# A linear-attention recurrence with a top-1 mixture of experts behind it: fewer matmuls of zeros, later weight splits, whole-block input loads, a new order at the seam

## The chip, the core and the metric

The kernel runs on one core of a Trainium2 chip. A core has five engines that run side by side: TensorE (PE in the profile, its weight loads PEld), VectorE (DVE), ScalarE (ACT), GpSimd (POOL) and SyncE (SP), which here only issues DMA transfers. The metric is the device time of one execution in microseconds (us), the median of the runs shown.

## The reference

Two layers follow one another. The first runs over time; the second sends each of the 3072 tokens to one of eight experts.

```python
B, H, S, D = 4, 8, 768, 48              # batch, heads, time, head width
for t in range(S):
    cur = einsum('bhd,bhe->bhde', u * k[t], v[t])
    y[t] = einsum('bhd,bhde->bhe', r[t], state + cur)
    state = w[t][..., None] * state + einsum('bhd,bhe->bhde', k[t], v[t])
x = y as [3072, 384]
logits = x @ w_gate                      # 8 experts
e = argmax(logits); gate = max(softmax(logits))
out[token] = gate * (relu(x @ w1[e]) @ w2[e])   # w1 384x1024, w2 1024x384
```

## The kernel before

**Blocks.** Time is cut into six chunks of 128 steps. A block is one chunk of one batch row, so there are 24 blocks, n = 0 to 23, chunk n // 4, batch row n % 4. The eight heads stand in pairs: partitions 0 to 47 hold the even heads and 64 to 111 the odd ones, so tiles have 112 rows (`RP`). `iteration(n)` issues a software pipeline on TensorE, VectorE, ScalarE and GpSimd, in an order that is written out by hand: products of decays by scans for block n+2 (`pre`, `suf`), from them `rh` and `kh` (VectorE), `rk` = r times k for block n+3 (GpSimd), the matrix `ap` = kh by rh for block n (`pe_a`), its causal part written into `at` (`dve_at`), the part of the state (`pe_inter`), the output (`pe_av`), the new state (`pe_state`), and for block n-1 the transposed output (`pe_y`). The loop runs over n = -3 to 21; the last two blocks, 22 and 23, are written out behind it.

**Matmuls of zeros.** `keep_warm` multiplies a tile of ones with a tile of zeros into a part of a bank that nobody reads. It stands ahead of the loop (`WARM`: 40 of 128 columns, 24 of 512), in `pe_coef` (384 columns) and in `pe_state` (320 columns).

**Routing.** When a chunk's four blocks are done, `logit_mm`, `gate`, `count`, `rank` and `place` find each token's expert and row, and `scatter` writes the rows to `xs` in DRAM, sorted by expert, by an indirect DMA from GpSimd for each block. For the last chunk this is done block by block (`pe_logits`, `gate`, `rank`, then `chosen` = place, weigh, scatter).

**Experts.** Weights are kept as a high and a low part (`split_piece`: ScalarE copies the high part, VectorE subtracts for the low one), and a product of two such numbers is three matmuls. An expert's weights come in four pieces of 128 by 1536; each piece is split in three parts of 512 columns. Expert 0 is split during the loop, one part per block from block 8 on (`split_piece(*lows[0], half="h")`, the low half one block later). Its first 192 tokens, the part `pa`, are worked on at the end of the recurrence: `load_rows`, three steps of `transpose_rows`, eight `mm1(f)`, then `mm2`. The other 256 tokens are the part `pb`: its rows can be loaded only when all scatters have landed. Then come experts 1 to 7, sorted by their token counts.

**Queues.** Every load is issued by SP in program order. A load waits for its buffer and stops all that stand behind it. The staging pool `wst` has three buffers, so a piece of weights can be loaded when the piece three before it has been split. Blocks of inputs go round a ring of six buffers (`ld`); from block 6 on, a block's w, r and k come in two transfers of 48 rows, which leave out the unused rows:

```python
for rs in ((slice(None),) if n < LD else (slice(0, D), slice(64, RP))):
    nc.sync.dma_start(t[rs], rkw[n][rs])
```

Of the kernel before, what the change touches and what calls it, by code (L numbers as in the profile page):

```python
# [19 lines left out]
P = 128  # L20
C = 128
# [6 lines left out]
NR = NP_ * C  # L28
NTOK = B * S
# [8 lines left out]
WARM = (40, 24)  # L38
# [7 lines left out]
def rwkv_moe_kernel(ctx, tc, rkw, vv, ub, wgp, wg, w1, w2, out):  # L46
# [26 lines left out]
    def load(n):  # L73
        if n >= NB:
            return

        if n < LD:
            ring.append(ld.tile([RP, NW + 2 * NR], F32, name="rkwt", tag="rkwt"))
        t = ring[n % LD]
        if n == 0:  # L80
            for cs in (slice(0, NW), slice(NW, NW + NR), slice(NW + NR, NW + 2 * NR)):
                nc.sync.dma_start(t[:, cs], rkw[n][:, cs])
        else:
            for rs in ((slice(None),) if n < LD else (slice(0, D), slice(64, RP))):
                nc.sync.dma_start(t[rs], rkw[n][rs])
        blk[n] = dict(
            w=t[:, 0:NW], r=t[:, NW:NW + NR].rearrange("p (q c) -> p q c", c=C),
            k=t[:, NW + NR:].rearrange("p (q c) -> p q c", c=C))

# [100 lines left out]
    def load_piece(e, i):  # L190
        st = (ld if (e, i) == (SECOND, 3) else wst).tile([P, 1536], F32, name="wst", tag="rkwt" if (e, i) == (SECOND, 3) else "wst")
        if i < 2:
            src = w1[e].rearrange("e (j p) (k f) -> p (e j) k f", p=P, f=512)
            for q in range(3):
                lin = 3 * i + q
                nc.sync.dma_start(st[:, q * 512:(q + 1) * 512], src[:, lin // 2, lin % 2, :])
        else:
            src = w2[e].rearrange("e (c p) d -> p (e c) d", p=P)
            nc.sync.dma_start(st.rearrange("p (c d) -> p c d", d=DM), src[:, 4 * (i - 2):4 * (i - 2) + 4, :])
        return st  # L200
# [13 lines left out]
    def w1v(t, pt, j, f):  # L214
        col = j * FF + f * P
        return t["w1", pt].rearrange("p a b -> p (a b)")[:, col:col + P]
# [44 lines left out]
    def transpose_rows(t, nq, rows, xh, xl):  # L261
        for j in range(3):
# [46 lines left out]
    def pool_rk(n):  # L309
        if real(n):  # L310
            d = blk[n]
            d["rk"] = wk.tile([RP, NP_, C], F32, name="rk", tag="rk", bufs=4)
            i = nc.gpsimd.tensor_tensor(out=d["rk"], in0=d["r"], in1=d["k"], op=ALU.mult)  # L313
# [47 lines left out]
    def dve_at(n):  # L361
        if real(n):
            d = blk[n]
            for j in range(2):
                nc.vector.copy_predicated(out=d["at"][:, j], mask=cmask.unsqueeze(1).broadcast_to([P, NP_, C]), data=d["ap"][j])  # L365
# [20 lines left out]
    def act_y(n):  # L386
        if real(n):
            d = blk[n]
            yt = ytb[n % NY]
            if n >= B:  # L390
                nc.scalar.activation(yt, d["yp"], AF.Copy)
# [31 lines left out]
    def pe_coef(n):  # L423

        if real(n):
            t = psL.tile([P, BANK], F32, name="cp", tag="lg")
            keep_warm(t[:, C:], 6 if n < B else 3 if n % B in (2, 3) else 1)
# [39 lines left out]
    def pe_state(n):  # L467
        if real(n) and n // B < NCH - 1:
# [3 lines left out]
            keep_warm(t[:, NP_ * D:], 6 if n < B else 2 if n % B < 2 else 0)  # L472
# [172 lines left out]
    def scatter(c, bs=range(B)):  # L645
        xr = ch["xr", c]
        for b in bs:
            i = nc.gpsimd.indirect_dma_start(out=xsf, out_offset=bass.IndirectOffsetOnAxis(ap=ch["pi", c, b], axis=0),  # L648
                                             in_=xr[:, b, :], in_offset=None, bounds_check=E * NTOK - 1, oob_is_err=False)
            for k in scat:  # L650
                tc.declare_no_dep(i.ins, k, reason="rows of different tokens")
            scat.append(i.ins)

            nc.gpsimd.memset(none, 0.0)
# [5 lines left out]
    class Part:  # L660
# [8 lines left out]
        def trans(self):  # L669
            weights(self.t)  # L670
            transpose_rows(self.t, 2, self.rows, self.x[0], self.x[1])
# [17 lines left out]
    lows = []  # L689

    def iteration(n):
# [7 lines left out]
        whole = (route, 0, B)  # L699
        act_y(n - 1)  # L700
# [5 lines left out]
        pool_rk(n + 3)  # L706
        if n in (6, 7):
            scatter(0, (2 * n - 12,))
# [4 lines left out]
        if n in (6, 7):  # L713
            scatter(0, (2 * n - 11,))
        if route > 0 and b > 1:
            scatter(route, (2 * b - 4, 2 * b - 3))
# [9 lines left out]
        dve_rh(n + 2)  # L726
        act_xr(n - 1)
# [15 lines left out]
        if n < NB - 3:  # L743
            dve_kh(n + 2)
        for k in lows:
# [6 lines left out]
        if route >= 0 and b == 1 and not last:  # L752
# [3 lines left out]
        if 0 <= m < 12:  # L756
# [12 lines left out]
        if n in (14, 17, 20, 21):  # L769
            stg[1, (14, 17, 20, 21).index(n)] = load_piece(SECOND, (14, 17, 20, 21).index(n))  # L770
# [104 lines left out]
    with tc.manual_schedule(engines={ET.PE, ET.DVE, ET.Activation, ET.Pool}):  # L875
# [9 lines left out]
        def chosen(i):  # L885
            place(each[i])
            weigh(each[i])
            scatter(lc, (i,))
# [3 lines left out]
        dve_at(n2)  # L892
        pool_diag(n3)
# [3 lines left out]
        dve_kh(n3)  # L897
        act_xr(n2 - 1)
        place((lc - 1, 0, B))
        scatter(lc - 1)  # L900
        pe_av(n2)
        act_y(n2)
        gate(each[0])
        count(each[0])
        pe_a(n3)
        pe_logits(n2 - 1)
        act_ex(each[0])
        pe_inter(n3)
        dve_at(n3)
# [4 lines left out]
        count(each[1])  # L914
        pe_av(n3)
        act_y(n3)
        act_ex(each[1])
        pe_logits(n2)
        chosen(0)
        pa.trans()  # L920
        rank(each[1])
        gate(each[2])
# [6 lines left out]
        banks = [(psA, "ap"), (psA, "ap"), (psK, "kp"), (psK, "kp")]  # L929
        pa.mm1(0)  # L930
# [5 lines left out]
        pa.mm1(1)  # L936
        pa.mm1(2)
        rank(each[3])
        chosen(3)
        pa.mm1(3)  # L940
        sort_experts()
        check_w()
        pa.mm1(4)
        pa.mm1(5)
        check()
# [3 lines left out]
        pa.mm1(6)  # L949
        pa.mm1(7)  # L950
# [35 lines left out]
def general(tc, rkw, vv, wg, w1, w2, out, xs, ident, tri, ones, ubt, iom, ebase, tokid, dram):  # L986
# [6 lines left out]
    with ExitStack() as st:  # L993
# [22 lines left out]
        with ExitStack() as s1:  # L1016
            gp = s1.enter_context(tc.tile_pool(name="g2", bufs=1))
            gps = s1.enter_context(tc.tile_pool(name="g2p", bufs=1, space=PSUM))
            with tc.For_i(0, NB, 1) as n:
                blk = bass.ds(n, 1)  # L1020
                t = gp.tile([RP, NW + 2 * NR], F32, name="grkw")
                nc.sync.dma_start(t, rkw[blk].rearrange("o p f -> p (o f)"))
# [150 lines left out]
```

## Time and profile before

| | |
|---|---|
| median of 3 runs | 431.68 us (431.0 to 433.52) |
| the profiled execution's own time | 432.07 us |
| its span, first to last instruction | 430.4 us |
| PE, PEld | 417.7 us (97%), 369.6 us (86%) |
| DVE, ACT, POOL | 272.7 us (63%), 222.2 us (52%), 130.1 us (30%) |
| mean granted TensorE clock | 0.973 of full speed |
| DMA | 62.62 MB, mean 146 GB/s |

The recurrence takes the first 168 us of the span, part `pa` and the end of the routing some 25 us behind it, and the rest are the experts. Busy shares are means over all of this; PE's records overlap, so that its share tells little by itself. The profiled execution is 0.39 us over the median.

### The profile page before, as it was taken

The numbers are of one execution on the slowest core, as the hardware profiler recorded it, in microseconds if no ns is written. First come the engines' busy times: TensorE is split into PE (matmuls) and PEld (weight loads), VectorE is DVE, ScalarE is ACT, GpSimd is POOL, SyncE is SP. The second block draws the span as 40 slices with busy tenths as digits, with TensorE's granted clock in tenths as the row PEclk, the third lists the DMA queues.
The fourth block names the chain that finished last, engine by engine and source line by source line (L and its number), as shares of the span: only waits on it lengthen the run. The fifth ranks groups of instructions, "written<-read, shape, count | busy, mean of one in ns | idle before, by whom it ended". The sixth has DMA issues, their size and how long they took to land.

```text
span 430.4 us, 9690 instructions
## 1 busy us (share of the span) xinstructions
PE 417.7 (97%) x3693; PEld 369.6 (86%) x3693; DVE 272.7 (63%) x499; ACT 222.2 (52%) x629; POOL 130.1 (30%) x160
## 2 busy tenths in 40 slices
PE   8999999999999998999999999999999999999994
PEld 5677778777777787989999988899999999999993
DVE  6999888998999974346874364364463562632321
ACT  4689687787887762135563353353363543421310
POOL 3654175463744634101010030031030071020432
PEclk9999999999999998579999999999999999999998
DMA  8999986885974152154862463454365435010021
GB/s 219 252 214 281 246 226 178 217 217 132 270 189 131 39 176 109 40 135 142 261 203 68 142 183 89 144 160 121 131 191 143 148 91 158 14 51 2 6 42 60
DMA packets 33179, 62.62 MB, mean 146 GB/s; under 512 B 8086, under 2 KB 21199, under 8 KB 33126
## 3 DMA queue, kind: packets, MB, share of 16 engines
q1 hardware_dynamic: 25222, 52.41, 44.9%
q0 software_dynamic: 7904, 9.52, 7.2%
q8 instruction: 31, 0.51, 0.6%
q14 instruction: 22, 0.18, 0.1%
HBM read 50.03 MB, written 12.29 MB: 145 GB/s over the span
## 4 chain that ended last, share of the span: by engine, by line
PE 54%; issue 34%; POOL 4%; DMA 3%; ACT 3%; DVE 1%; POOLq 0%; ACTq 0%
PE bank L274 10%; PE ap L452 5%; PE yp L464 5%; PE yp L488 5%; POOL out_dram L236 4%; PE opt L291 4%; DMA out_dram<-ot,xg 3%; PE yq L495 3%; PE bank L859 3%; PE dp L479 2%; PE kp L443 2%; PE cp L111 2%; PE wrm L111 2%; PE cp L429 2%; PE cpt L435 2%
## 5 line engine op out<-in xcount | busy, mean ns | idle before, releaser
L236 POOL DMA_INDIRECT out_dram<-ot,xg x24 | 35.2, 1469 | 157.2 <-DVE ot L849 151.7
L212 DVE TENSOR_TENSOR w2l<-wst,w2h 128x512 fp32r<-128x512 f32 x48 | 31.5, 686 | 44.3 <-ACT w2h L210 44.1
L274 PE MATMUL bank<-xl,w1h 128*128 128x448 f32 (+6 forms) x168 | 59.0, 355 | 0.0
L274 PE MATMUL bank<-xh,w1l 128*128 128x448 f32 (+6 forms) x168 | 58.2, 352 | 0.0
L274 PE MATMUL bank<-xh,w1h 128*128 128x448 f32 (+6 forms) x168 | 55.7, 359 | 0.6 <-ACT xh L266 0.3
L277 DVE SCALAR_TENSOR_TENSOR hl<-bank,hh 128x192 fp32r<-128x192 f32 (+8 forms) x58 | 30.5, 540 | 36.3 <-ACT hh L276 36.3
L313 POOL TENSOR_TENSOR rk<-rkwt 112x512 f32<-112x512 f32 x24 | 32.8, 1368 | 65.5 <-DVE suf L344 48.0
L276 ACT ACTIVATE hh<-bank 128x192 fp32r<-128x192 f32 (+8 forms) x58 | 26.6, 477 | 47.3 <-PE bank L274 43.5
L864 ACT ACTIVATE oT<-bank 128x448 f32<-128x448 f32 (+5 forms) x18 | 9.4, 525 | 61.6 <-PE bank L859 61.6
L859 PE MATMUL bank<-hl,w2h 128*128 128x412 f32 (+5 forms) x114 | 40.6, 358 | 0.0
L859 PE MATMUL bank<-hh,w2l 128*128 128x412 f32 (+5 forms) x114 | 40.4, 356 | 0.0
L859 PE MATMUL bank<-hh,w2h 128*128 128x412 f32 (+5 forms) x114 | 40.0, 357 | 0.0
L365 DVE COPY_PREDICATED at<-cmask,ap 128x512 f32<-128x512 int32 x48 | 32.4, 727 | 9.6 <-PE ap L452 7.1
L350 DVE TENSOR_TENSOR_SCAN suf<-rkwt,suf 112x520 f32<-112x520 f32 x24 | 33.6, 1398 | 0.0
L648 POOL DMA_INDIRECT xs<-xr,pi x24 | 27.6, 1149 | 19.6 <-DVE xr L553 6.9
L274 PEld LDWEIGHTS bank<-xh,w1h 128*128 128x128 f32 x168 | 31.2, 188 | 2.2 <-ACT xh L266 0.7
L274 PEld LDWEIGHTS bank<-xl,w1h 128*128 128x128 f32 x168 | 31.6, 188 | 1.1
L274 PEld LDWEIGHTS bank<-xh,w1l 128*128 128x128 f32 x168 | 31.5, 188 | 1.1
L341 DVE TENSOR_TENSOR_SCAN pre<-rkwt,preone 112x520 f32<-112x520 f32 x24 | 30.9, 1289 | 2.4 <-DMA rkwt<-in_rkw_dram 2.4
L210 ACT ACTIVATE w1h<-wst 128x512 fp32r<-128x512 f32 x48 | 28.2, 629 | 8.0 <-PE bank L274 7.9
L212 DVE TENSOR_TENSOR w1l<-wst,w1h 128x512 fp32r<-128x512 f32 x48 | 30.9, 686 | 1.1 <-PE bank L274 0.6
L335 ACT ACTIVATE at<-ident,ct 128x128 f32<-128x128 f32 x96 | 30.9, 416 | 0.0
(162 smaller groups left out, 924.3 us busy)
## 6 DMA issues: line engine op xcount, KB each, us to landing
wst<-in_w_dram SPq DMA_DIRECT2D x48, 256.0 KB, 3.5
wst<-in_w_dram SPq DMA_DIRECT2D x16, 768.0 KB, 6.4
rkwt<-in_rkw_dram SPq DMA_DIRECT2D x36, 289.5 KB, 7.3
vt<-in_vv_dram SPq DMA_DIRECT2D x24, 192.0 KB, 5.9
rkwt<-in_rkw_dram SPq DMA_DIRECT2D x5, 675.5 KB, 14.1
xg<-xs SPq DMA_DIRECT2D x5, 579.0 KB, 5.4
xs<-zrow SPq DMA_DIRECT2D x8, 289.5 KB, 6.7
xg<-xs SPq DMA_DIRECT2D x2, 675.5 KB, 5.6
```

The costliest lines, as they stand in the source:

```text
L210: nc.scalar.activation(hi, st[:, cs], AF.Copy)
L212: nc.vector.tensor_tensor(out=lo, in0=st[:, cs], in1=hi.bitcast(F32), op=ALU.subtract)
L236: i = nc.gpsimd.indirect_dma_start(out=out[:, :], out_offset=bass.IndirectOffsetOnAxis(ap=t.bitcast(I32)[:, q, DM + 1:DM + 2], axis=0), in ...
L274: nc.tensor.matmul(hp, a, x[:, j, :], start=(i == 0), stop=(i == 8))
L277: nc.vector.scalar_tensor_tensor(out=hl, in0=hp, scalar=0.0, in1=hh.bitcast(F32), op0=ALU.max, op1=ALU.subtract)
L313: i = nc.gpsimd.tensor_tensor(out=d["rk"], in0=d["r"], in1=d["k"], op=ALU.mult)
L335: nc.scalar.activation(blk[n]["at"][:, 1, q], ident, AF.Copy, scale=blk[n]["ct"][:, 2 * q + 1:2 * q + 2])
L341: nc.vector.tensor_tensor_scan(out=pre, data0=d["w"], data1=preone.rearrange("p q c -> p (q c)"), initial=0.0, op0=ALU.mult, op1=ALU.add)
L350: nc.vector.tensor_tensor_scan(out=suf[:, ::-1], data0=d["w"][:, ::-1], data1=suf0[n % 2].rearrange("p q c -> p (q c)")[:, ::-1], initial= ...
L365: nc.vector.copy_predicated(out=d["at"][:, j], mask=cmask.unsqueeze(1).broadcast_to([P, NP_, C]), data=d["ap"][j])
L648: i = nc.gpsimd.indirect_dma_start(out=xsf, out_offset=bass.IndirectOffsetOnAxis(ap=ch["pi", c, b], axis=0), in_=xr[:, b, :], in_offset=No ...
L859: nc.tensor.matmul(pp, w, a, start=(i == 0), stop=(i == 23))
```

## The change

Six edits are made at once.

- **Zeros.** `pe_coef` and `pe_state` issue no matmuls of zeros from block 4 on; ahead of the loop 12 of 512 columns are left instead of 24.
- **Weights of expert 0.** Only the first piece is split in the loop (blocks 8 to 10). The other nine parts are split behind it, one at a time, by `split_more()` between the steps of the routing and `mm1`. w1 is cut otherwise, so that piece 0 serves `mm1(0)` to `mm1(3)`. The loads of the next expert's first three pieces, whose buffers these are, move behind the splits.
- **Scatters.** Not two in a row in an iteration any more, but spread by two tables over the iterations; chunk 4 is placed in the loop, and its four scatters are tied to steps of blocks 22 and 23.
- **Inputs.** One transfer of 128 rows for each block, from an array that is padded to 128 rows and a row length of 1600 elements.
- **rk.** For blocks 0 to 2 on VectorE, not GpSimd.
- **The last two blocks.** The transpositions of `pa`, its first `mm1` and the routing steps stand in another order.

```diff
-WARM = (40, 24)
+WARM = (40, 12)
...
         if n < LD:
-            ring.append(ld.tile([RP, NW + 2 * NR], F32, name="rkwt", tag="rkwt"))
+            ring.append(ld.tile([P, NT], F32, name="rkwt", tag="rkwt"))
...
-            for rs in ((slice(None),) if n < LD else (slice(0, D), slice(64, RP))):
-                nc.sync.dma_start(t[rs], rkw[n][rs])
+            nc.sync.dma_start(t, rkw[n][:, 0:NT])
+        t = t[:RP]
...
-                nc.sync.dma_start(st[:, q * 512:(q + 1) * 512], src[:, lin // 2, lin % 2, :])
+                nc.sync.dma_start(st[:, q * 512:(q + 1) * 512], src[:, lin % 3, lin // 3, :])
...
-            keep_warm(t[:, C:], 6 if n < B else 3 if n % B in (2, 3) else 1)
+            keep_warm(t[:, C:], 6 if n < B else 0)
...
-            keep_warm(t[:, NP_ * D:], 6 if n < B else 2 if n % B < 2 else 0)
+            keep_warm(t[:, NP_ * D:], 6 if n < B else 0)
...
+    before = {8: [(0, 1)], 9: [(0, 3)]}
+    after = {7: [(0, 0)], 8: [(0, 2)]}
+    for c in range(1, NCH - 2):
+        after[B * c + 6] = [(c, 0)]
+        after[B * c + 7] = [(c, 1)]
+        before[B * c + 8] = [(c, 2)]
+        after[B * c + 8] = [(c, 3)]
...
-        pool_rk(n + 3)
-        if n in (6, 7):
-            scatter(0, (2 * n - 12,))
+        if n >= 0:
+            mul_rk(n + 3, nc.gpsimd)
...
+        if n < 0:
+            mul_rk(n + 2, nc.vector)
...
+        if n == -1:
+            mul_rk(2, nc.vector)
...
         m = n - 8
-        if 0 <= m < 12:
+        if 0 <= m < 3:
             lows.append((wt0, stg[0, m // 3], m // 3, 3, m % 3))
...
-        if n in (14, 17, 20, 21):
-            stg[1, (14, 17, 20, 21).index(n)] = load_piece(SECOND, (14, 17, 20, 21).index(n))
+        if n == 21:
+            stg[1, 3] = load_piece(SECOND, 3)
...
+        later = [(i, p) for i in range(1, 4) for p in range(3)]
+
+        def split_more():
+            i, p = later.pop(0)
+            split_piece(wt0, stg[0, i], i, 3, p)
+            if p == 2:
+                stg[1, i - 1] = load_piece(SECOND, i - 1)
```

**TensorE, in the loop.** The end of an iteration with n % 4 = 1: `kp` is the transposed kh of the next block, `dp` the new state, `cpt` the coefficients of block n+2, `yp` the output. Before:

```order
L443 MATMUL kp<-ident,kh 128x112 x4
L111 LDWEIGHTS ones
L111 MATMUL dp<-wz,ones 128x320
L111 LDWEIGHTS ones
L111 MATMUL dp<-wz,ones 128x320
L474 MATMUL dp<-sst_194,ident 112x192
L479 MATMUL dp<-vt,kt 48x48 x8
L435 MATMUL cpt<-pick,cs 128x8
L488 MATMUL yp<-at,vt 48x128 x8
```

Now:

```order
L445 MATMUL kp<-ident,kh 128x112 x4
L476 MATMUL dp<-sst_182,ident 112x192
L481 MATMUL dp<-vt,kt 48x48 x8
L437 MATMUL cpt<-pick,cs 128x8
L490 MATMUL yp<-at,vt 48x128 x8
```

The two matmuls of zeros are gone, and nothing has taken their place. From block 4 on, 40 of 384 columns and 16 of 320 go in this way.

**VectorE, behind the loop.** The steps around the sorting of the experts (`all`, `key`, `ks`, `ki`, `order`) and the check of the decays (`g`, `gm`, `gb`); `hl` is the low part of one `mm1`, which frees its bank, `w2l` the low part of weights. Before:

```order
L277 SCALAR_TENSOR_TENSOR hl<-bank,hh 128x192
L604 TENSOR_REDUCE all<-cn 1x1
L605 SCALAR_TENSOR_TENSOR key<-cn,iom 1x6
L608 MAX ks<-key 1x8
L610 CAST ki<-ks 1x8
L611 TENSOR_SCALAR order<-ki 1x8
L614 COPY c_3050<-cn 1x2
L619 TENSOR_SCALAR g<-wtot 112x24x4
L620 TENSOR_SCALAR g<-chk 112x24
L622 TENSOR_REDUCE gm<-g 112x1
L624 CAST gb<-gm 112x1
L277 SCALAR_TENSOR_TENSOR hl<-bank,hh 128x192 x2
```

Now, from the same place to `gb` and on to the next split:

```order
L616 COPY c_2950<-cn 1x2
L214 TENSOR_TENSOR w2l<-wst,w2h 128x512
L279 SCALAR_TENSOR_TENSOR hl<-bank,hh 128x192
L621 TENSOR_SCALAR g<-wtot 112x24x4
L622 TENSOR_SCALAR g<-chk 112x24
L624 TENSOR_REDUCE gm<-g 112x1
L626 CAST gb<-gm 112x1
L214 TENSOR_TENSOR w2l<-wst,w2h 128x512
L279 SCALAR_TENSOR_TENSOR hl<-bank,hh 128x192
L214 TENSOR_TENSOR w2l<-wst,w2h 128x512
```

A split now stands ahead of nearly every `hl`; all nine are between the last transposition of `pa` and its last `hl`, where there was none.

**SP, behind the loop.** `wst` of 128x512 and 128x4x384 are pieces of weights, `xg` of 96x772 the rows of `pa`, `xg` of 128x772 the rows of `pb`, `xg` of 112x1544 those of expert 1. Before, from the load of block 23's inputs on:

```order
L85 DMA rkwt<-in_rkw_dram 48x1544 x2
L94 DMA vt<-in_vv_dram 128x384
L196 DMA wst<-in_w_dram 128x512 x3
L94 DMA vt<-in_vv_dram 128x384
L199 DMA wst<-in_w_dram 128x4x384
L230 DMA xg_2649<-xs 96x772
L199 DMA wst<-in_w_dram 128x4x384
L230 DMA xg_3147<-xs 128x772
L230 DMA xg<-xs 112x1544
```

Now:

```order
L86 DMA rkwt<-in_rkw_dram 128x1544
L96 DMA vt<-in_vv_dram 128x384 x2
L232 DMA xg_2538<-xs 96x772
L201 DMA wst<-in_w_dram 128x4x384
L198 DMA wst<-in_w_dram 128x512 x6
L201 DMA wst<-in_w_dram 128x4x384
L232 DMA xg_3061<-xs 128x772
L232 DMA xg<-xs 112x1544
```

Three pieces of expert 1 have moved from the loop to a place between the rows of `pa` and the rows of `pb`. The last of them, ahead of `xg_3061`, waits for the ninth split.

## Rows read from the trace of the kernel before

**Rows 1.** Windows: each engine's busy us (instructions), granted clock, DMA share, GB/s.

```profile
30.00:40.00 10.00, 9.80 (x141) 7.68 (x133) 9.90 (x13) 9.08 (x32) 4.12 (x4) 1.00 1.04 277
112.00:124.00 12.00, 11.95 (x184) 9.18 (x181) 11.76 (x16) 9.81 (x35) 6.63 (x8) 1.00 1.04 264
160.00:168.00 8.00, 7.25 (x88) 5.99 (x82) 3.92 (x18) 2.82 (x9) 5.33 (x10) 1.00 0.34 125
170.00:188.00 18.00, 18.00 (x87) 17.72 (x88) 5.96 (x38) 2.83 (x10) 3.13 (x6) 0.50 0.33 93
184.00:186.00 2.00, 2.00 (x11) 2.00 (x11) 1.32 (x12) 0.23 (x2) 0.00 (x0) 0.50 1.02 320
```

**Rows 2.** Timeline of TensorE in the loop: start, duration, line, operation [idle before].

```profile
88.35 0.33 PE L111 MATMUL cp<-wz,ones 128*128 128x384 bf16 x1
88.61 0.42 PE L429 MATMUL cp<-rk,ubt 112*32 112x128 f32 x8
...
91.65 1.16 PE L452 MATMUL ap<-rh,kh 64*128 64x128 f32 x16
...
94.29 0.65 PE L111 MATMUL cp<-wz,ones 128*128 128x384 bf16 x3
94.88 0.43 PE L429 MATMUL cp<-rk,ubt 112*32 112x128 f32 x8
...
96.74 0.43 PE L111 MATMUL dp<-wz,ones 128*128 128x320 bf16 x2
97.01 0.49 PE L474 MATMUL dp<-sst,ident 112*112 112x192 f32 x2
...
112.15 1.16 PE L452 MATMUL ap<-rh,kh 64*128 64x128 f32 x16
...
118.09 1.16 PE L452 MATMUL ap<-rh,kh 64*128 64x128 f32 x16
```

**Rows 3.** Waits of VectorE, 40 to 150 us: total, times, longest.

```profile
DVE at L365 <- PE ap L452: 5.3, 7, 1.2
```

**Rows 4.** Timeline of VectorE in the loop.

```profile
111.86 1.23 DVE L341 TENSOR_TENSOR_SCAN pre<-rkwt,preone 112x520 f32<-112x520 f32 x1
...
118.27 1.23 DVE L341 TENSOR_TENSOR_SCAN pre<-rkwt,preone 112x520 f32<-112x520 f32 x1
```

**Rows 5.** Groups by line: a split's low half (total us, mean ns | idle before).

```profile
L212 DVE TENSOR_TENSOR w1l<-wst,w1h 128x512 fp32r<-128x512 f32 x48 | 30.9, 686 | 1.1 <-PE bank L274 0.6 <-ACT w1h L210 0.3
```

**Rows 6.** Timeline of VectorE at the start.

```profile
10.20 1.24 DVE L341 TENSOR_TENSOR_SCAN pre<-rkwt,preone 112x520 f32<-112x520 f32 x1 [1.50 <-DMA rkwt<-in_rkw_dram]
...
17.54 1.34 DVE L365 COPY_PREDICATED at<-cmask,ap 128x512 f32<-128x512 int32 x2
```

**Rows 7.** Timeline of TensorE from block 22 to the part pb.

```profile
156.64 1.16 PE L452 MATMUL ap<-rh,kh 64*128 64x128 f32 x16
...
165.16 1.06 PE L596 MATMUL lg<-wgt,ytb 112*128 112x8 f32 x8
...
187.51 0.52 PE L291 MATMUL opt<-w2h,hh 128*96 128x384 f32 x1
...
192.25 0.60 PE L265 MATMUL pt<-ident,xg 128*128 128x128 f32 x4
...
198.19 0.40 PE L274 MATMUL bank<-x,w1h 128*128 128x256 f32 x2
...
199.24 0.40 PE L274 MATMUL bank<-x,w1h 128*128 128x256 f32 x2
```

**Rows 8.** The chain that ended last, one piece: two mm1 of pa.

```profile
173.32 3.99 PE bank L274 x18
```

**Rows 9.** Timeline of VectorE behind the loop.

```profile
173.46 0.36 DVE L277 SCALAR_TENSOR_TENSOR hl<-bank,hh 128x192 fp32r<-128x192 f32 x1 [4.05 <-ACT hh L276]
...
180.33 0.14 DVE L604 TENSOR_REDUCE all<-cn 1x1 f32<-1x8 f32 x1
...
181.74 0.16 DVE L624 CAST gb<-gm 112x1 bf16<-112x1 f32 x1
```

**Rows 10.** Timeline of SP: the loads of the rows of pb and of expert 1.

```profile
182.01 0.81 SPq L230 DMA_DIRECT2D xg<-xs  x2
```

## What the change will do to the time

> **What bounds the kernel now.** I read the windows first, because the busy shares of the table are means over three different stretches. In the loop [rows 1] TensorE is busy 11.95 of 12.00 us at 112 to 124, at a granted clock of 1.00, and VectorE 11.76. The reader is to see two engines that are both nearly full. Which of them sets the pace is told by who waits: VectorE loses 5.3 us in the 110 us from 40 to 150 by waiting for `ap` at `dve_at` [rows 3], 1.3 us in a chunk, while TensorE's rows stand end to start [rows 2]. So TensorE is the bound, by about 1.3 us a chunk. A chunk of four blocks takes 118.09 - 91.65 = 26.44 us [rows 2]. At 30 to 40 it is nearer still (9.80 to 9.90).
>
> At the seam the picture changes. From 160 to 168 TensorE is busy 7.25 of 8.00; from 170 to 188 it is busy 18.00 of 18.00, but at a clock of 0.50 (1.2 GHz of 2.4), and VectorE 5.96 [rows 1]. Nine matmuls of one `mm1` take 2.0 us there (3.99 for two) [rows 8], and 1.05 at full clock (199.24 - 198.19) [rows 7]. A busy TensorE at half speed bounds the seam. Behind it the experts bound themselves, and the change leaves them alone. I therefore cut the sum in three: start, loop, and the seam from `pe_a(22)` at 156.64 to the first transposition of `pb` at 192.25, that is 35.61 us [rows 7].
>
> **The loop.** The row of three zeros in `pe_coef` stands 0.59 us ahead of its successor, that of one 0.26, that of two in `pe_state` 0.27 [rows 2]. I take these steps, not the longer durations, since matmuls overlap. A chunk of iterations has two of each: 2.24 us. Iterations 4 to 19 make 4 x 2.24 = 8.96, and iterations 20 and 21 issue the three-column kind for blocks 22 and 23: 1.18. Gross: -10.1. The zeros of iterations 2 and 3 lie in a stretch where VectorE sets the pace; I count them at nothing.
>
> Does VectorE then take over? Its block with one split takes 118.27 - 111.86 = 6.41 us without a gap [rows 4]; a split's low half is 0.69 [rows 5]. Nine of the twelve leave the loop, so a block without one takes 5.72, a chunk 22.9, against TensorE's new 26.44 - 2.24 = 24.20. VectorE has 1.3 us to spare, unless a split stays: in blocks 8 to 10 three do, 22.9 + 2.1 = 25.0 at most against 24.20. That costs between 0.4 (if VectorE's 22.4 from 26.44 - 1.3 - 4 x 0.69 holds) and 2.1; I take 1.2. The blocks are not even either: a light one of TensorE needs 118.09 - 112.15 = 5.94 [rows 2], less a zero of 0.26 that is 5.68, the same as VectorE's 5.72, and what either waits for in one block it does not get back in the next. I take 0.9 for it, with bounds of nothing and 3. **Loop: -8.0, bounds -5 and -10.**
>
> Costed at nothing here: the scatters that move by an iteration or two (GpSimd was busy 6.63 of 12.00 [rows 1]), and the larger loads, 0.79 MB for 0.59 a block, which are issued some three blocks, 17 us, ahead. What hides them is that lead; if the lead goes, 0.20 MB at 277 GB/s cost 0.7 us a block. At 30 to 40 the DMA share is already 1.04 [rows 1], so this cover is thinnest early.
>
> **The start.** The first `at` is at 17.54, and the chain to it is VectorE's, from the landing of block 1's inputs at 10.20 [rows 6]. So 12 fewer zeros in the warm-up give nothing. The inputs of the first six blocks grow by 14% (112 to 128 rows), which brings the landing at 10.20 up to 1.0 us later if bytes set it, nothing if latency does. Three products `rk` move to VectorE; the two nearest rows are the split of 0.69 [rows 5] and nothing, if they fit the gap of 1.50 [rows 6]. **Start: +0.3, bounds -0.5 and +1.5.**
>
> **The seam**, counted from `pe_a(22)` as 0. TensorE's end of `pe_av(23)` stays at 165.16 - 156.64 = 8.52 [rows 7]. What is now ahead of it are three transposition steps of `pa` (half of the four in 0.60 each [rows 7]), say 0.8, and a wait for a bank that a copy frees, for which I take 0.75 (between nothing and two passes of 0.69): 10.1. Then come two passes of ScalarE, a copy and the split's high half, at some 0.65 each by the low half on the same tile, and that low half, 0.69 [rows 5]: 12.1. Now VectorE has eight more splits (8 x 0.69 = 5.5), eight `hl` (8 x 0.36 = 2.9) and, by the order of its instructions, some 41 small steps of routing, sorting and checks; ten of these stand in 180.33 to 181.74 plus the last's 0.16, 0.157 each [rows 9], so 6.4. That makes 14.8 without a gap, of which only the last `hl` stands behind the ninth split: it ends near 26.6. Before, VectorE was busy 5.96 of 18.00 there [rows 1]: it had the room, and now it is nearly full.
>
> SP is queued behind that split. Its load of expert 1's third piece waits for the buffer that the ninth split frees, and the rows of `pb` stand right behind it on the queue. Before, the load of these rows was issued at 182.01 [rows 10], 25.4 after `pe_a(22)`, and nothing of the kind stood ahead of it. Two transfers, 0.79 and 0.40 MB, at the 320 GB/s of 184 to 186 [rows 1] are 3.7 us, and I add 1.4 from issue to the first bytes: the rows are there at 26.6 + 5.1 = 31.8 (rounded).
>
> TensorE itself would be ready earlier or later according to its clock. If the clock stays at 1.00, eight `mm1` of 1.05 end with VectorE's last `hl` near 25 to 26.6, and `mm2` takes at most the 4.74 us from 187.51 to 192.25 [rows 7]: about 30. If it falls to 0.50 as it did, eight `mm1` of 2.0 from 12.1 end at 28.1, and with 4.74 `pb` starts at 32.8. The clock fell behind a stretch with routing's matmuls of 8 columns and little else, and this stretch is still there, only mixed with transpositions and `mm1(0)`; so I take 32.8. Gain 35.61 - 32.8 = 2.8. **Seam: -2.8, bounds -1.1 (VectorE's small steps wait for TensorE and GpSimd, some 1.7 more) and -6.3 (full clock, and the rows' bytes early).**
>
> The Trainium skill, page "TensorE: Matmul & The Clock Gate", Part 1, "What's actually happening", has it that the throttled state is the default and "activity releases the throttle". By that, the busy TensorE of the seam should have been at full clock; here it stayed at 0.50 while busy 18.00 of 18.00 [rows 1], so busy time alone isn't the activity, and the trace decides. By the rule the seam would be 31.8, limited by `pb`'s rows, and the total 1.0 less.
>
> **Sum.** 432.07 of the profiled execution, -8.0, +0.3, -2.8: 421.6. It lies 0.39 over the median of the runs, so I predict 421.2.
>
> **Rivals.** *B: the seam stays fast.* Clock at 1.00 and `pb`'s rows there before TensorE wants them: the other bound of the seam, -6.3, which is 3.5 more: 417.7. For it: transpositions and an `mm1` now stand between the small matmuls. Against: the queue behind the ninth split.
>
> *C: VectorE or GpSimd becomes the bound.* VectorE and TensorE differ by 1.3 us a chunk [rows 3], and every uneven block eats of it. If only half of the loop's gain is left (-4.0) and the seam gives its lower bound (-1.1): 432.07 - 4.0 + 0.3 - 1.1 - 0.4 = 426.9. For it: 11.76 of 12.00 [rows 1]. Against: the nine splits that go are just what makes VectorE full.
>
> *S: little change.* TensorE now waits where it issued zeros, for other engines that go round at the old pace, and the seam only moves its wait to `pb`'s rows: some -1 in all, 430.5. Against it: TensorE's rows without idle time [rows 2].
>
> *D: slower.* The zeros hold the clock up. The loop ran at 1.00 with them [rows 1]; without them the same rows of TensorE have fewer columns, and the only fall of the clock in this trace came behind a stretch with few columns. A block at half clock takes up to 2.0/1.05 = 1.9 times as long: 5.68 becomes 10.8, +5.1. The forecast's gain of 10.5 is gone at 2.1 such blocks; a fall that lasts one chunk gives 421.2 + 20.4 = 441.6. Against it: the blocks with one row of zeros already ran at 1.00 for two iterations in a row, and in the shorter period the share of real work rises. The page named above speaks for D: what is removed is activity. In this trace the loop at 1.00 with zeros bears it out no further than that it doesn't contradict it.
>
> **How the numbers follow.** A measurement of this kernel tells about 0.5% (2.2 us) from no change. Chances: the forecast 0.55, with its own range 418 to 425 (the loop's bounds, with the start's); B 0.14; C 0.17; S 0.06; D 0.08. D is slower, S and a strip of C's upper end are the same (0.07), the rest is faster (0.85). The range must reach to B and C and may leave out D, S and the far ends: 415.5 (B with a loop of -10) to 427.5 (C and a little more).
>
> **What the profile after would show.** Right: a chunk of 24.2 to 24.7 us between two `pe_a` four blocks apart at clock 1.00; `pe_a(22)` near 149; first `at` near 17.8; the last low half of `w2l` of expert 0 some 26 us behind `pe_a(22)`, then the load of `pb`'s rows, and `pb`'s first transposition at 32 to 33. Wrong in the loop: TensorE idle for VectorE's `kh`, `rh` or `at`, or for ScalarE's copies. Wrong at the seam: the chain of waits runs over the splits of VectorE (C) or never leaves TensorE at clock 1.00 (B). Wrong altogether: a granted clock of 0.50 anywhere ahead of block 22.

## The result and the profile after

The changed kernel took 427.4 us (median of four, 425.17 to 434.43), the one before 432.15; the ratio is 0.9881 with a 95% interval of 0.9832 to 0.9929, about 5.1 us less. One of the four, 434.43, ran at a mean granted clock of 0.953 (the others 0.965 to 0.982), and the ratio leaves it out. Forecast were 421.2 us, 10.5 less. The range to 427.5 just holds the time, but the gain is a little under half of what was forecast. The profiled execution took 425.17 (span 423.5) and is the fastest of them, with the highest mean clock; the rows below are read from it.

Where the 6.9 us of span went is seen by cutting both profiles at the starts of `ap`. The table is worked out from these starts; "seam" runs from `pe_a(22)` to `pb`'s first transposition.

| us | before | after | early scatters (below) |
|---|---|---|---|
| first `ap` | 15.39 | 13.14 | 13.32 |
| blocks 0 to 4 | 23.70 | 23.37 | 23.37 |
| blocks 4 to 8 | 26.22 | 24.36 | 24.36 |
| blocks 8 to 12 | 26.34 | **32.25** | 24.49 |
| blocks 12 to 16 | 26.44 | 24.27 | 24.34 |
| blocks 16 to 20 | 26.08 | 23.84 | 23.85 |
| blocks 20 to 22 | 12.47 | 11.42 | 11.89 |
| seam | 35.61 | 31.37 | 37.97 |
| behind it | 238.15 | 239.48 | 238.81 |

Every chunk does what was forecast but one. Blocks 12 to 16, the first rows of which are these on TensorE, take 117.39 - 93.12 = 24.27 us, 2.17 less than in [rows 2]:

```profile
93.12 1.16 PE L454 MATMUL ap<-rh,kh 64*128 64x128 f32 x16
...
117.39 1.16 PE L454 MATMUL ap<-rh,kh 64*128 64x128 f32 x16
```

Windows of the changed kernel around blocks 9 and 10 (columns as in [rows 1]) show a hole, and behind it a clock that before never fell in the loop:

```profile
70.00:72.00 2.00, 2.00 (x29) 1.37 (x28) 2.00 (x3) 0.79 (x3) 2.00 (x4) 1.00 0.94 225
72.00:74.00 2.00, 0.55 (x17) 0.42 (x16) 2.00 (x2) 0.00 (x0) 1.28 (x3) 1.00 1.01 311
74.00:76.00 2.00, 0.00 (x0) 0.00 (x0) 1.93 (x6) 0.00 (x0) 0.00 (x0) 1.00 0.90 374
76.00:78.00 2.00, 0.47 (x2) 0.47 (x2) 1.37 (x3) 1.16 (x4) 0.65 (x2) 0.70 0.00 0
78.00:80.00 2.00, 2.00 (x19) 1.60 (x19) 0.00 (x0) 1.49 (x5) 0.76 (x1) 0.50 0.04 8
80.00:82.00 2.00, 2.00 (x19) 1.78 (x20) 0.00 (x0) 1.95 (x8) 1.69 (x3) 0.50 0.37 95
```

From 74 to 76 TensorE, ScalarE and GpSimd all stand still while the DMA engines are busy 0.90. Who waits for whom stands in the timelines. First TensorE, then ScalarE, then GpSimd:

```profile
77.53 0.59 PE L437 MATMUL cpt<-pick,cs 128*128 128x8 f32 x2 [4.98 <-ACT cs L410]
78.05 1.95 PE L490 MATMUL yp<-at,vt 128*48 128x128 f32 x16
79.93 2.08 PE L454 MATMUL ap<-rh,kh 64*128 64x128 f32 x16
...
69.50 1.29 ACT L337 ACTIVATE at<-ident,ct 128x128 f32<-128x128 f32 x4
76.75 0.55 ACT L405 ACTIVATE xr<-yq 128x192 f32<-128x192 f32 x2 [5.96 <-DMA xs<-xr,pi]
77.19 0.28 ACT L410 ACTIVATE cs<-cp 128x128 f32<-128x128 f32 x1
...
67.57 1.86 POOL L649 DMA_INDIRECT xs<-xr,pi  x1 [0.17 <-issue]
69.73 0.99 POOL L649 DMA_INDIRECT xs<-xr,pi  x1 [0.21 <-issue]
```

Read from the bottom: the last scatter of chunk 0 starts at 69.73 (in iteration 9, where the new table puts it). ScalarE's copy `xr` of block 8 waits 5.96 us for a scatter's DMA. `xr` has two buffers, one per chunk, so chunk 2 writes into the buffer that the scatters of chunk 0 read. Behind this copy on ScalarE stands `cs`, and for `cs` TensorE waits 4.98. The chain of waits has the scatter's landing, the time from its issue until its data are there, as its longest piece:

```profile
69.73 6.92 DMA xs<-xr,pi
...
76.75 0.55 ACT xr L405 x2
```

With the wait the clock falls: `ap` takes 2.08 for 1.16. Blocks 9 and 10 take 12.31 and 7.41 where 6.18 and 5.78 are possible, 7.8 us in all.

At the seam the load of `pb`'s rows stands where it was forecast, behind the piece for which the ninth split has to end. VectorE's split, SP's two loads and TensorE's first transposition of `pb`:

```profile
177.19 0.67 DVE L214 TENSOR_TENSOR w2l<-wst,w2h 128x512 fp32r<-128x512 f32 x1
...
177.89 0.38 SPq L201 DMA_DIRECT2D wst<-in_w_dram  x1
178.63 0.80 SPq L232 DMA_DIRECT2D xg<-xs  x2
...
184.02 0.66 PE L267 MATMUL pt<-ident,xg 128*128 128x128 f32 x4 [1.48 <-DMA xg<-xs]
```

The rows arrive 31.4 us behind `pe_a(22)` (152.65), and TensorE waits 1.48 for them. Windows: the clock fell only at the end of the eight `mm1`, not ahead of them as in [rows 1], and once more behind the wait for the rows:

```profile
160.00:168.00 8.00, 7.36 (x73) 6.76 (x74) 3.78 (x17) 4.32 (x13) 2.95 (x7) 1.00 0.21 75
174.00:176.00 2.00, 1.50 (x13) 1.50 (x14) 1.97 (x8) 0.19 (x1) 0.00 (x0) 0.95 0.91 276
176.00:178.00 2.00, 2.00 (x11) 1.91 (x11) 1.82 (x13) 0.99 (x3) 0.00 (x0) 0.50 0.60 223
...
186.00:188.00 2.00, 2.00 (x9) 1.73 (x8) 1.68 (x5) 1.81 (x4) 0.00 (x0) 0.51 0.89 329
```

The part behind the seam is 1.3 us longer. Half of that, 0.7, lies ahead of TensorE's last matmul (232.6 us from `pb`'s first transposition on, for 232.0), in the stretch with this second fall. The other half lies behind that matmul (6.9 for 6.2), where TensorE's clock can't be the cause.

### The profile page after: what moved, and what is told of

Its sections match the earlier page's. It is cut to its first block, busy times and chain, and to the rows that moved or that the text cites. A ratio compares the mean times of both kernels' runs of the same rounds, so it can differ in the third digit from the quotient of the medians.

```text
span 423.5 us, 9521 instructions
## 1 busy us (share of the span) xinstructions
PE 402.5 (95%) x3624; PEld 360.0 (85%) x3625; DVE 272.1 (64%) x502; ACT 222.7 (53%) x629; POOL 124.8 (29%) x157
## 4 chain that ended last, share of the span: by engine, by line
PE 86%; ACT 4%; DVE 3%; DMA 3%; issue 2%; POOL 1%; POOLq 0%; SPq 0%; ACTq 0%
PE bank L276 24%; PE bank L874 20%; PE opt L293 6%; PE ap L454 5%; PE yp L466 5%; PE yp L490 5%; PE yq L497 3%; PE pt L267 2%; PE dp L481 2%; PE kp L445 2%; PE cp L431 2%; PE op L863 2%; PE cpt L437 2%; DMA xs<-xr,pi 2%; PE wrm L113 2%
## 5 line engine op out<-in xcount | busy, mean ns | idle before, releaser
L214 DVE TENSOR_TENSOR w2l<-wst,w2h 128x512 fp32r<-128x512 f32 x48 | 31.4, 685 | 44.4 <-ACT w2h L212 44.1
L278 ACT ACTIVATE hh<-bank 128x192 fp32r<-128x192 f32 (+8 forms) x58 | 26.6, 477 | 37.3 <-PE bank L276 36.6
L279 DVE SCALAR_TENSOR_TENSOR hl<-bank,hh 128x192 fp32r<-128x192 f32 (+8 forms) x58 | 30.3, 537 | 24.2 <-ACT hh L278 24.0
L315 POOL TENSOR_TENSOR rk<-rkwt 112x512 f32<-112x512 f32 x21 | 27.0, 1286 | 54.0 <-DVE suf L346 43.7
L649 POOL DMA_INDIRECT xs<-xr,pi x24 | 28.7, 1194 | 18.3 <-issue 7.0
L343 DVE TENSOR_TENSOR_SCAN pre<-rkwt,preone 112x520 f32<-112x520 f32 x24 | 29.6, 1232 | 0.7 <-DMA rkwt<-in_rkw_dram 0.7
## 6 DMA issues: line engine op xcount, KB each, us to landing
xg<-xs SPq DMA_DIRECT2D x2, 675.5 KB
```

Source lines behind the costliest of these rows:

```text
L214: nc.vector.tensor_tensor(out=lo, in0=st[:, cs], in1=hi.bitcast(F32), op=ALU.subtract)
L279: nc.vector.scalar_tensor_tensor(out=hl, in0=hp, scalar=0.0, in1=hh.bitcast(F32), op0=ALU.max, op1=ALU.subtract)
L315: i = eng.tensor_tensor(out=d["rk"], in0=d["r"], in1=d["k"], op=ALU.mult)
L343: nc.vector.tensor_tensor_scan(out=pre, data0=d["w"], data1=preone.rearrange("p q c -> p (q c)"), initial=0.0, op0=ALU.mult, op1=ALU.add)
```

## The experiments

The theory: the hole in block 9 is the landing of chunk 0's last scatter, for whose buffer `xr` waits. Its rivals: the larger loads that fill the DMA engines at 72 to 76 stop the engines by themselves; or the clock falls for want of zeros and drags the rest along. Ratios are to the kernel before on the same chip; the changed kernel's is 0.9881.

### The wait in block 9

**Early scatters** (all of the change, with chunk 0 scattered where it was).

```diff
-    before = {8: [(0, 1)], 9: [(0, 3)]}
-    after = {7: [(0, 0)], 8: [(0, 2)]}
+    before = {}
+    after = {6: [(0, 0), (0, 1)], 7: [(0, 2), (0, 3)]}
```

> The changed kernel, but chunk 0 is scattered where it was before (two in iteration 6, two in 7, instead of 7, 8, 8 and 9). Landing theory: in block 9 the copy of xr for chunk 2 waits for the last scatter of chunk 0, whose buffer it takes, and everything behind it on ScalarE waits too. Then the four blocks 8 to 12 take 24.2 to 24.8 us instead of 32.25, the clock stays at 1.00 from 64 to 90, and the time falls by 7 to 8 us to about 419.5 (ratio to before near 0.971). Rival, contention: the larger loads at 68 to 76 us stop ScalarE and GpSimd whatever the scatters do; then a wait of 3 to 5 us stays in blocks 9 to 10, and the time stays above 424. Rival, clock: without zeros the clock falls in that stretch by itself; then it is 0.50 for some us though no wait stands ahead of it.

Measured: 0.9709 (0.9657 to 0.9760), 418.6 us. Blocks 8 to 12 take 24.49 us, and the window has no hole and no fall of the clock:

```profile
64.00:90.00 26.00, 25.92 (x421) 20.77 (x412) 25.62 (x39) 21.11 (x77) 16.30 (x18) 1.00 0.70 225
```

The larger loads are the same here, so they don't stop the engines by themselves, and without zeros the clock holds. The profiled execution of this run took 424.17, its longest time: the seam is 37.97 there, and its clock was at 0.50 from 154 to 178; more on that below. The wait itself is not gone for good: later chunks' copies of `xr` still wait for a scatter, 1.38 us in block 13 and 1.26 in block 21 of this profile.

**Three buffers for xr**, scatters as late as in the changed kernel.

```diff
-    xrp = actx.enter_context(tc.tile_pool(name="xrp", bufs=2))
+    xrp = actx.enter_context(tc.tile_pool(name="xrp", bufs=3))
```

> The changed kernel with three buffers for the rows xr instead of two; the scatters stay late. Landing theory: the copy of xr for chunk 2 finds a free buffer, so the wait of 5 us at block 9 goes and the time is that of the run with early scatters, near 419.5, to within 1 us. If lateness of GpSimd or the loads were the cause and not the buffer, the wait stays, and the time is near 427.

Measured: 0.9721 (0.9680 to 0.9763), 419.4 us; blocks 8 to 12 in 24.89. The scatters come as late as before (the last of chunk 0 took 7.8 us to land), and nobody waits for them, here or in any later chunk. With the run above this shows the buffer to be the cause.

**Late scatters alone**, in the kernel before.

```diff
-        if n in (6, 7):
-            scatter(0, (2 * n - 12,))
...
+        if n in (8, 9):
+            scatter(0, (2 * n - 15,))
         act_y(n - 1)
...
-        if n in (6, 7):
-            scatter(0, (2 * n - 11,))
+        if n in (7, 8):
+            scatter(0, (2 * n - 14,))
```

> The kernel before, only with chunk 0 scattered in iterations 7, 8, 8 and 9 as in the changed kernel; zeros, loads and splits as before. Landing theory: the same wait appears at block 9 to 10, of 1 to 5 us (the scatter lands 3.4 to 7 us behind its issue), so +1 to +7 us, 433 to 439. Contention theory: with the smaller loads of before the scatter lands in time and nothing is lost, 432.

Measured: 0.9987 (0.9936 to 1.0039): no difference that can be told, though the wait is there. The landing, from the chain of waits, and ScalarE's row:

```profile
73.42 5.73 DMA xs<-xr,pi
...
79.25 0.55 ACT L403 ACTIVATE xr<-yq 128x192 f32<-128x192 f32 x2 [2.77 <-DMA xs<-xr,pi]
```

The wait is 2.77 us, and block 9 takes 8.05 for 6.95: 1.1 us lost, without a fall of the clock. So the edit costs little in the slower loop and 7.8 in the faster one. The waits differ by 5.96 - 2.77 = 3.19. Of this, 1.2 is the landing (6.92 for 5.73). The larger part, 2.0, is that ScalarE was ready for the copy sooner: 1.06 us behind the start of the scatter (76.75 - 5.96 - 69.73) where it is 3.06 here (79.25 - 2.77 - 73.42). That the larger loads make the landing slower is likely from these two profiles, and was not tried by itself.

### Zeros and splits

**Zeros removed alone**, in the kernel before.

```diff
-            keep_warm(t[:, C:], 6 if n < B else 3 if n % B in (2, 3) else 1)
+            keep_warm(t[:, C:], 6 if n < B else 0)
...
-            keep_warm(t[:, NP_ * D:], 6 if n < B else 2 if n % B < 2 else 0)
+            keep_warm(t[:, NP_ * D:], 6 if n < B else 0)
```

> The kernel before, only without the zeros from block 4 on. The term of the prediction, -8.0 (bounds -5 and -10): chunks of 24.2 to 24.7 us and a time of about 424 (ratio near 0.981). Theory that the zeros' time comes out in full once nothing else stands in the way: -8 to -10, even though nine more splits stay on VectorE; if VectorE takes over in the blocks with a split (12 of them), chunks of 25 us and -5 to -6. Rival, clock: the granted clock falls to 0.50 somewhere in the loop and the gain is lost, 430 or more.

**All but the zeros**: the version with early scatters, and the two lines above put back.

> The version with early scatters and the zeros of before back in the loop: all of the change but the zeros (ahead of the loop 12 stay). Theory that zeros and splits go together: with the splits behind the loop but the zeros there, TensorE sets the pace at 26.2 to 26.5 us a chunk, 8 to 9 us more than without the zeros, so some 426 if the seam keeps its clock. Clock theory: with the zeros the clock holds through the last blocks, the seam is the same or shorter, and part of the 9 us comes back: 420 to 424, with less spread between runs.

Measured: 0.9956 (0.9906 to 1.0007) and 0.9966 (0.9892 to 1.0039). Neither alone gives anything that can be told; the whole of the change with early scatters gives 2.9%. The second run also holds the edits to the start and the seam, so the two are no clean pair, and I read the loop's rows. One window of each, zeros removed first:

```profile
120.00:150.00 30.00, 28.88 (x447) 22.66 (x447) 29.59 (x44) 23.11 (x83) 20.17 (x23) 1.00 0.40 116
```

```profile
120.00:150.00 30.00, 29.50 (x462) 23.35 (x461) 25.56 (x42) 21.93 (x80) 14.72 (x21) 1.00 0.21 73
```

Without zeros but with a split in each block VectorE is full (29.59), and a chunk from block 8 on takes 25.3 to 25.6 us, 0.5 to 1.0 less than in the kernel before. 2.6 us were lost again in block 7 (8.24 for 5.68), where GpSimd began the first scatter late, at 62.11 after 6.53 us idle, and TensorE waited for what stood behind it. With zeros but without nine of the splits TensorE is full and VectorE has 4.4 us to spare; a chunk from block 4 on takes 25.7 to 26.7, where the kernel before has 26.1 to 26.4. Each edit takes work off one of two engines that were level.

### The start

Three undos on the version with early scatters: `WARM = (40, 24)`; the inputs in transfers of 112 rows, then of twice 48; `mul_rk` on GpSimd for all blocks.

```diff
-WARM = (40, 12)
+WARM = (40, 24)
```

```diff
-            nc.sync.dma_start(t, rkw[n][:, 0:NT])
+            for rs in ((slice(0, RP),) if n < LD else (slice(0, D), slice(64, RP))):
+                nc.sync.dma_start(t[rs], rkw[n][rs, 0:NT])
```

```diff
-        if n >= 0:
-            mul_rk(n + 3, nc.gpsimd)
+        mul_rk(n + 3, nc.gpsimd)
...
-        if n < 0:
-            mul_rk(n + 2, nc.vector)
...
-        if n == -1:
-            mul_rk(2, nc.vector)
```

> The version with early scatters and the 24 zeros of 512 columns ahead of the loop that the kernel before has, not 12. TensorE theory: each of its instructions at the start stood 2.25 us earlier in the changed kernel, as long as its first coefficients stood right behind the zeros; then the first ap stands at 15.4 again and 2.0 to 2.3 us are lost (about 420.8). VectorE theory, that of the prediction: the zeros give nothing, since VectorE's chain from the landing of block 1's inputs sets the first at; then the loss is below 0.5 us.

> The version with early scatters and the input transfers of before in shape: 112 rows for the first six blocks, then two transfers of 48 rows a block. If the whole-block transfers bring the inputs sooner (772 KB landed in 6.1 us in the changed kernel, 675.5 KB in 14.1 us before), VectorE waits for block 1's inputs again, the first at is 1 to 2.5 us later and the time 1.5 to 2.5 us higher, and the DMA share of the first 64 us is back over 1.0. If the bytes count, as the prediction had it, the start is up to 1 us earlier and the time the same or 0.5 lower.

> The version with early scatters and rk of blocks 0 to 2 on GpSimd as before. If the two engines slow each other, kh of the first blocks takes 1.57 us again beside rk on GpSimd (0.69 without), rk 2.2, and the first at is 1 to 2 us later; if the move is neutral, as the prediction had it, the time is within 0.5 us.

Measured: 0.9796 (0.9733 to 0.9859), 0.9836 (0.9773 to 0.9899) and 0.9779 (0.9714 to 0.9844), where early scatters alone have 0.9709 (0.9657 to 0.9760). Only the interval of the second lies clear of that, and the times are blurred by the clock at the seam, so I read the rows. The start varies from profile to profile, though: eight profiles share the changed kernel's start, and in them the first `ap` stands at 13.08 to 15.04 and the first `at` at 15.09 to 17.25 (13.32 and 15.88 in the version that the three undos are made from). In the three profiles with the old start these are 15.39 to 16.14 and 17.54 to 19.02.

More zeros: TensorE's warm-up is 9.38 us (6.23 to 7.86 in the profiles with 12 zeros), `ap` stands at 15.73, later than in any of the eight, and VectorE waits for it:

```profile
1.30 9.38 PE L113 MATMUL wrm<-wz,ones 128*128 128x128 bf16 x63 [1.30 <-POOL cmask L133]
...
15.73 1.16 PE L454 MATMUL ap<-rh,kh 64*128 64x128 f32 x16
...
16.99 0.73 DVE L367 COPY_PREDICATED at<-cmask,ap 128x512 f32<-128x512 int32 x1 [1.12 <-PE ap L454]
```

Narrow inputs: the DMA engines move less. Windows of the first 16 us, the changed kernel first, show 340 and 234 GB/s at the same DMA share; the ten profiles with 128 rows have 311 to 340. Then the landing of the large transfers issued in this stretch:

```profile
0.00:16.00 16.00, 13.82 (x120) 9.56 (x122) 14.04 (x25) 10.40 (x30) 2.62 (x11) 1.00 0.90 340
```

```profile
0.00:16.00 16.00, 12.72 (x108) 9.05 (x109) 12.19 (x22) 9.61 (x28) 2.34 (x10) 1.00 0.90 234
```

```profile
rkwt<-in_rkw_dram SPq DMA_DIRECT2D x7, 772.0 KB, 8.4
...
rkwt<-in_rkw_dram SPq DMA_DIRECT2D x5, 675.5 KB, 14.4
```

The 6.1 us that the expectation sets against 14.1 is the median of all 23 large transfers of the changed kernel, most of them later ones; like for like it is 8.4.

But VectorE waits for block 1 until 10.23, where the eight have 8.26 to 10.47, and `at` stands at 16.81, within their range. So this profile does not show a later start:

```profile
10.23 1.24 DVE L344 TENSOR_TENSOR_SCAN pre<-rkwt,preone 112x520 f32<-112x520 f32 x1 [1.73 <-DMA rkwt<-in_rkw_dram]
```

These inputs come with a wait of 3.5 us of `xr` for a scatter, in block 13 (9.79 us). `rk` on GpSimd: `kh` takes 1.57 us beside it and 0.69 without:

```profile
6.87 1.57 DVE L361 TENSOR_TENSOR kh<-rkwt,suf 112x512 f32<-112x512 f32 x1
...
6.03 1.87 POOL L315 TENSOR_TENSOR rk<-rkwt 112x512 f32<-112x512 f32 x1 [4.16 <-DMA rkwt<-in_rkw_dram]
```

The Trainium skill, page "SBUF — State Buffer", section "Who interferes with whom", says that a VectorE instruction with two SBUF inputs contends with a GpSimd instruction that reads SBUF; these two rows agree. The first `at` stands at 15.80, though, no later than the 15.88 of the version without this undo: what `kh` gains, the three products on VectorE take. So the start came forward by some 2 us, the zeros are shown to hold it back when they are put in again, and what the other two edits are worth there stays open.

### The seam

**pb's rows first**: the load of expert 1's third piece moves from the ninth split to behind `pb = Part(...)`, in the version with early scatters.

```diff
-            if p == 2:
+            if p == 2 and i < 3:
                 stg[1, i - 1] = load_piece(SECOND, i - 1)
...
         pb = Part(HA, HB // 2)
+        stg[1, 2] = load_piece(SECOND, 2)
```

> The version with chunk 0's early scatters, and the load of expert 1's third piece moved behind the load of pb's rows. The prediction's queue theory of the seam: pb's rows stood behind 768 KB of weights that wait for the ninth split; taken off, TensorE's wait for the rows before the first transposition of pb (1.48 us in the changed kernel's profile) goes, and the time falls by 1 to 2 us against the version with early scatters (418.6). Rival: the rows wait for the last scatter of chunk 5, issued near 173, and land no earlier; then the wait stays and the time is the same. Second rival: the piece itself, 2 us later, makes the experts wait later on, and the gain is given back.

> Early scatters, three buffers for xr and pb's rows ahead of expert 1's third piece. Landing theory: the waits of xr for a scatter (1.3 to 2.4 us at block 21 in the profiles with two buffers) are gone for good, and with them some of the falls of the clock in the last blocks: 415 to 417, at or below the 417.1 of the version with two buffers. If the clock falls there without any wait, as in the profile of the run with three buffers, the spread stays and the median is about 417 to 419.

Measured: 0.9677 (0.9618 to 0.9736), and with three buffers for `xr` besides 0.9626 (0.9554 to 0.9698), 415.8 us; against early scatters alone (0.9709, 0.9657 to 0.9760) neither can be told apart by its interval. In the second's profile SP issues the first of `pb`'s two loads at 168.79, ahead of the piece at 170.59, and TensorE's transposition follows without a wait:

```profile
168.79 0.33 SPq L232 DMA_DIRECT2D xg<-xs  x1
170.59 0.38 SPq L201 DMA_DIRECT2D wst<-in_w_dram  x1
...
175.06 0.60 PE L267 MATMUL pt<-ident,xg 128*128 128x128 f32 x4
```

The seam is 29.81 us there and the part behind it 237.34: the wait of 1.48 is gone, and the clock did not fall again right behind the seam. No copy of `xr` waits for a scatter in this profile. This version, 3.7% under the kernel before and some 2.6% under the changed one by the two ratios, is the one to keep.

**The check of the decays behind the last mm1**, in that version. The release of the recurrence's buffers, which stands behind the check, moves with it.

```diff
         split_more()
-        check()
...
         pa.mm1(7)
+        check()
```

> The version of best0, and the check of the decays, for whose one small matmul TensorE waited 1.50 us in the changed kernel's profile, stands behind the last mm1 of pa. If that wait is on the path: 1 to 1.5 us less than best0. If the ninth split or pb's rows end last there, the same as best0.

Measured: 0.9613 (0.9537 to 0.9689). TensorE's wait of 1.50 (1.49 in that version) is gone from the profile, but the time is the same. The profile can't tell what the wait was worth: its clock was near 0.50 from 158 to 169, in that version's only from 168 to 172, and the seam is 30.25 for 29.81. The runs at a mean clock of 0.994 and 0.995 took 414.50 and 414.47 us, two of that version at 0.994 took 414.16 and 414.66.

**Zeros at the seam**, in that version.

```diff
-            keep_warm(t[:, C:], 6 if n < B else 0)
+            keep_warm(t[:, C:], 6 if n < B else 3 if n >= NB - B else 0)
...
-        lg = psK.tile([P, 1, E], F32, name="lg", tag="kp")
+        t = psK.tile([P, BANK], F32, name="lg", tag="kp")
+        keep_warm(t[:, C:], 2)
+        lg = t[:, 0:E].unsqueeze(1)
```

> The version of best0 with zeros where TensorE's work is thin: three of 384 columns ahead of the coefficients of blocks 20 to 23 as in the kernel before, and two ahead of each block's routing matmuls. They cost up to 4 x 0.59 + 5 x 0.33 = 4 us at full clock. Clock theory: the clock stays at 1.00 to the end of the recurrence (granted mean 0.985 to 0.995 in all runs), the slow runs of 422 and more vanish, and the median is at or below best0's though the fastest run is 2 to 4 us slower. Rival: the fall of the clock has nothing to do with the zeros; then the median is 3 to 4 us above best0's and the spread is the same.

Measured: 0.9625 (0.9546 to 0.9703). Five of its seven runs have a mean granted clock of 0.993 to 0.998 (414.7 to 418.0 us), two have 0.961 and 0.966 (428.2 and 426.3). The version without them had six runs of 414.2 to 418.9 at 0.982 to 0.994. So these zeros don't keep the clock up in every run; whether they help at all stays open.

## Why the prediction was wrong

- **The failed step is "Costed at nothing here: the scatters that move by an iteration or two (GpSimd was busy 6.63 of 12.00 [rows 1])".** I looked for room on the engine that issues the scatters. The price is set by who waits for their landing: `xr`'s two buffers make the copy in iteration 9 wait for the last scatter of chunk 0, issued in that same iteration. In the changed kernel it cost 7.8 us (32.25 against 24.49), of it 4.98 as the wait and the rest mostly as the low clock behind it. With the scatters put back the ratio is 0.9709, 419.6 us on the scale of this kernel's 432.15, 1.6 under the forecast.
- **The loop's term was right.** -8.0 was forecast from `pe_a(0)` to `pe_a(22)`; with early scatters it is 132.30 against 141.25, -8.95. The zeros give 1.9 to 2.2 a chunk (2.24 by the steps of [rows 2]). The 1.2 for the three splits that stay were 0.3 (24.49 against 24.2), and the 0.9 for uneven blocks was not seen. That VectorE would take over unless the splits go was right too (25.3 to 25.6 us a chunk with them).
- **The start had the wrong sign.** +0.3 was forecast for the first `at`, -2.45 came (15.09 for 17.54; the first `ap` -2.25). "The inputs of the first six blocks grow by 14%", up to 1.0 later, failed: VectorE used block 1 at 8.26 to 10.47 in the profiles with the new start (8.26 in the changed kernel), at 10.20 to 11.60 in the three with the old one, and the first 16 us moved 340 GB/s for 229. "So 12 fewer zeros in the warm-up give nothing" holds only while VectorE's chain ends last; with this chain earlier, 12 more zeros make VectorE wait 1.12. The products on VectorE take their 0.68 each, and `kh` gives back 0.88.
- **The seam's rows came as forecast, but the prediction took the other bound.** `pb`'s rows, held up by the ninth split, were forecast at 31.8 and came at 31.4. Two errors offset each other there: the split ended at 25.2 for 26.6, and from its end to the rows it was 6.1 for 5.1, of which the 1.4 from issue to first bytes stood on no row. Forecast as last was TensorE at half clock, 32.8. In this profile the clock stayed up until 175, TensorE was ready at 29.9, and the rows bound it: -4.2 for -2.8. That is luck: in six of the later profiles the clock was near 0.50 for most of the seam, which took 37.4 to 40.1 us, more than the 35.6 of the kernel before and not 32.8. With early scatters the stretch of the eight `mm1` took 19.5 us at half clock (158.28 to 177.74) where the prediction gave it 16, as matmuls of the routing stand between them. Not foreseen: behind the wait for the rows the clock fell again, in a stretch that is 0.7 us longer than before.
- **That the total lies in the range is luck in part.** From the first `ap` to `pe_a(22)` the changed kernel gained 1.7 (139.51 for 141.25) where 8.0 were forecast; start and seam together gained 4.0 more than forecast.
- **Rivals.** B (the seam stays fast) came half: the clock stayed up in this profile, but the rows came after TensorE wanted them. C (a second engine becomes the bound) did not happen with the splits gone. D (the clock falls in the loop without zeros) happened in the changed kernel only behind the wait: its other chunks ran at 1.00. That rival named a fall without a cause; the cause was a stall of 5 us. For the last blocks D is not settled. In three of the ten profiles without zeros there the clock fell in block 21, in two of them behind a wait of `xr` for a scatter (TensorE waited 1.49 and 1.11), in the one with three buffers without it; in none of the four with zeros there did it fall in these blocks.

**Open.** Why the last scatter took 6.9 us to land; what the first scatter waited 4.3 us for at 62.5 ("issue" in the profile); and what lets the clock fall in blocks 21 to 23 in some runs. In the profile with three buffers it fell at 146 to 148 with no wait of half a microsecond on TensorE's matmuls ahead of it, where small matmuls of the routing stand:

```profile
144.00:146.00 2.00, 1.75 (x25) 1.05 (x25) 1.97 (x6) 1.46 (x8) 0.67 (x2) 1.00 0.16 26
146.00:148.00 2.00, 1.95 (x20) 1.60 (x22) 2.00 (x6) 1.06 (x4) 0.56 (x1) 0.70 0.87 269
```

## What to carry to other kernels

When a transfer that reads a buffer is moved later, look up who writes that buffer next and what stands behind the writer on its engine; that wait, not the issuing engine's load, is the price, and a third buffer is the cheap test: it removed the wait in every chunk, the earlier scatters only in one. A loop that is made faster reaches such a wait sooner and pays more for it: 2.0 of the 3.2 us by which the two waits differ. Where two engines are level, take work off both in one step: either edit alone gave no difference in time that could be told. A stall of a few microseconds costs more than itself if the clock falls behind it, here 7.8 us for a wait of 4.98.

## What was not expected of the hardware

In the first 16 us, transfers of 772 KB over 128 rows landed in 8.4 us (median of seven) in the changed kernel and in 9.6 with early scatters; transfers of 675.5 KB over 112 rows landed in 14.1 in the kernel before and in 14.4 in the version with narrow inputs. The DMA engines were busy 0.89 to 0.90 in all four and moved 340, 332, 229 and 234 GB/s. In the last of these the array is the padded one, so that only the rows (112, then twice 48) differ from early scatters. A `kh` on VectorE took 0.69 us alone and 1.57 beside `rk` on GpSimd. After a stall of 5 us the granted clock was 0.50 for about 6 us, and a block that takes 5.78 took 7.41.
